# A 34th slot for weight pieces and their high parts, and DMA scratch of 256 bytes

## The chip, the cores and the metric

The kernel runs on one core of a Trainium2 chip. The metric is the device time of one execution in microseconds (us). The kernel before took 749.93 us, the median of three runs (749.84 to 750.58). Every time below is of the kernel before.

## What is computed

An attention layer whose keys are limited to a local window and a few global positions, followed by a feed-forward layer with a rational activation. All tensors are f32:

```python
# q, k, v: (4 batches, 8 heads, 768 positions, 64)
rel = pos[:, None] - pos[None, :]
is_global = pos[None, :] < 8
is_local = (rel >= 0) & (rel < 96)
scores = q @ k.T / 8 - slope[head] * dist        # dist = |rel|, or 96 where only global
a = softmax(where(is_global | is_local, scores, -1e9))
x = (a @ v), heads side by side                  # 3072 tokens x 512
h = x @ w_in                                     # 512 x 2048
P = a0 + a1*h + a2*h**2 + a3*h**3
Q = 1 + |b0|*|h| + |b1|*h**2
out = (P / (Q + 1e-6)) @ w_out                   # 2048 x 512
```

## The kernel before

**Tiling.** The 3072 tokens are taken in 12 chunks of 256. A chunk needs 8 attention units (a unit is one block of 128 queries with one pair of heads) and 8 feed-forward steps f (a step is 256 of the 2048 hidden columns, as two halves of 128). Steps f = 0 to 7 belong to the first chunk, f = 8 to 15 to the second, and so on up to 95. Attention runs ahead of the feed-forward by 10 to 13 units, so that in the steady part each turn of the loop holds one attention unit and one feed-forward step of an earlier chunk.

**Two kinds of arithmetic on TensorE.** For the first chunk, TensorE multiplies with the plain f32 weights (h at L263, acc at L342). From the second chunk on, each weight and each activation is split in a high part, rounded to fp32r, and a low part, the remainder, and a product is three fp32r matmuls: high by high, high by low, low by high (h at L271, acc at L347). Attention's later units (u >= 24) use fp32r as well; the earlier ones, and the products with v (o, L520), stay f32.

**Weights.** `w_in` and `w_out` are cut in 32 pieces of 128x512. A piece goes through four stations:

- `fetch` loads its bytes into a raw tile (r).
- `decode` puts it together as f32 in a slot of the pool `wide`: an Abs on ScalarE (L202), a small scaling on GpSimd (L206), two bit operations on VectorE (L207, L209). The result is named `w_..f` in the trace. The table `WSCHED` says in which turn each piece is decoded (turns 0 to 16).
- `split_w` rounds it into a second slot of `wide`, `w_..h` (L222): every even one on VectorE, every odd one on ScalarE.
- `split_w` then subtracts (L223) and stores the low part in `win_l` or `wout_l`, which have room of their own. This runs on GpSimd, and for ten of the pieces on VectorE.

**The slots.** `wide` has `NCT * DF // (2 * TOK) + NFT + 1` = 16 + 16 + 1 = 33 slots of 128x512 f32, handed out in turn. 32 pieces and 32 high parts pass through them in the order in which the code asks: pieces 0 to 29, the high parts of 0 and 1, pieces 30 and 31, then the high parts of 2 to 31. So piece 31 takes the slot of piece 0, and the high part of piece n (n >= 2) the slot of piece n-1. It may be written only when everything that reads piece n-1 is done: the f32 matmuls of the first chunk and the subtraction of L223. The high part of n+1 waits in the same way for piece n, and so on: one chain through all pieces. The pieces' order is that of `WSCHED`: (1,2,0), (1,3,0), (1,0,0), (1,1,0), (1,2,1), (1,3,1), (1,0,1), (1,1,1) of `w_in`, then rows 0 to 3 of `w_out`, and so on to row 15.

**What sets the order of the work.** Every group of instructions has a priority: its turn, and within the turn a number from a table (`PRI`, in the first turns `PRI_A`). Splits come last in their turn (`wsplit`). A list scheduler with a timing model then lays down each engine's queue: at each point it takes the group of best priority among those which the model says can start. The queues are in order on the chip, so an instruction that waits holds up everything behind it on its engine.

**The feed-forward step on the engines.** h (TensorE) -> three activations from h (ScalarE, L295 to L297: fu, fa, fs) -> fu times h twice (VectorE, L302, L303) and fa + fs (GpSimd, L304) -> log and exp (ScalarE, L311, L312) -> three operations (VectorE, L316 to L318), whose last gives fu. In the first chunk acc (L342) reads fu. After it, ScalarE rounds fu into g (L326), GpSimd stores the remainder in g (L327), and acc (L347) reads g. The PSUM tiles of h are two, so the h of f waits until L303 of f-2 is done. GpSimd also scales the probabilities (L478, two for each unit).

**DMA scratch.** `dynamic_dma_scratch_size` keeps 2048 bytes of each partition of SBUF for transfers whose descriptors software makes.

## Time and profile before

| what | value |
|---|---|
| median of 3 runs | 749.93 us |
| the profiled execution | 750.29 us |
| its span, first to last instruction | 748.4 us |
| outside the span | 1.9 us |
| mean granted TensorE clock | 0.996 |
| TensorE busy, matmuls | 724.8 us |
| splits, high parts (L222) | 32, from 75.7 to 177.2 us |
| splits, low parts (L223) | 22 on GpSimd, 10 on VectorE, from 80.2 to 178.9 us |

The splits thus fill the second and third tenth of the execution. Up to about 115 us TensorE works on the first chunk in f32; the steady part with its three fp32r matmuls for each product begins near 140 us and goes on to the end. A matmul's record lasts longer than its share of the array, since one begins before the other has drained: what TensorE spends on it is read from one start to the next.

### The profile page before, as it was taken

The numbers are of one execution on the slowest core, as the hardware profiler recorded it, in microseconds if no ns is written. First come the engines' busy times: TensorE is split into PE (matmuls) and PEld (weight loads), VectorE is DVE, ScalarE is ACT, GpSimd is POOL, SyncE is SP. The second block draws the span as 40 slices with busy tenths as digits, with TensorE's granted clock in tenths as the row PEclk, the third lists the DMA queues.
The fourth block names the chain that finished last, engine by engine and source line by source line (L and its number), as shares of the span: only waits on it lengthen the run. The fifth ranks groups of instructions, "written<-read, shape, count | busy, mean of one in ns | idle before, by whom it ended". The sixth has DMA issues, their size and how long they took to land.

```text
span 748.4 us, 15330 instructions
## 1 busy us (share of the span) xinstructions
PE 724.8 (97%) x5026; PEld 629.8 (84%) x5026; DVE 601.4 (80%) x1437; ACT 576.9 (77%) x1303; POOL 456.4 (61%) x504
## 2 busy tenths in 40 slices
PE   5898999999999999999999999999999999999996
PEld 4575667888988989999999999998988989998995
DVE  5889965888889797878888888887888888876565
ACT  6898576977987886877877878777877877866674
POOL 3384996776576675665756657656666566664441
PEclk9999999999999999999999999999999999999999
DMA  9986101123534443334434334334434333210000
GB/s 259 306 277 224 48 22 23 50 52 99 146 103 126 151 121 94 113 108 101 119 94 120 113 101 125 107 101 106 124 93 124 117 86 107 74 50 1 29 1 33
DMA packets 123581, 79.49 MB, mean 106 GB/s; under 512 B 82532, under 2 KB 104036, under 8 KB 123492
## 3 DMA queue, kind: packets, MB, share of 16 engines
q1 hardware_dynamic: 122288, 77.89, 36.4%
q8 instruction: 42, 0.69, 0.4%
q10 hardware_dynamic: 1204, 0.52, 0.3%
q14 instruction: 47, 0.39, 0.2%
HBM read 35.92 MB, written 6.29 MB: 56 GB/s over the span
## 4 chain that ended last, share of the span: by engine, by line
PE 90%; DVE 3%; DMA 3%; ACT 1%; issue 1%; SPq 0%; POOL 0%; DVEq 0%; ACTq 0%
PE h L271 34%; PE acc L347 32%; PE o L520 5%; PE s L438 5%; PE tp L494 4%; PE acc L342 3%; PE h L263 3%; PE s L433 2%; PE tk L383 1%; DMA r<-in_moe_w_in_dram 1%; DMA r<-in_moe_w_out_dram 1%; PE tk L389 1%; DMA nat<-in_q_dram 0%; DVE pr L452 0%; ACT pr L462 0%
## 5 line engine op out<-in xcount | busy, mean ns | idle before, releaser
L478 POOL TENSOR_SCALAR pr<-pr,stats 128x256 f32<-128x256 f32 (+1 forms) x176 | 156.3, 899 | 74.8 <-DVE stats L469 42.7
L271 PE MATMUL h<-xh,win_l 128*128 128x256 f32 x704 | 198.2, 282 | 0.0
L304 POOL TENSOR_TENSOR fa<-fa,fs 128x512 f32<-128x512 f32 x95 | 123.5, 1300 | 98.0 <-ACT fs L297 85.3
L347 PE MATMUL acc<-wout_l,g 128*128 128x512 f32 x352 | 139.3, 396 | 0.0
L271 PEld LDWEIGHTS h<-xh,win_l 128*128 128x128 f32 x704 | 133.1, 189 | 2.1 <-issue 1.2
L327 POOL TENSOR_TENSOR g<-fu,g 128x512 fp32r<-128x512 f32 x87 | 113.9, 1310 | 34.2 <-ACT g L326 22.8
L295 ACT ACTIVATE fu<-h,coef 128x512 f32<-128x512 f32 (+1 forms) x97 | 74.9, 772 | 45.0 <-PE h L271 39.8
L462 ACT ACTIVATE pr<-pr,stats 128x256 f32<-128x256 f32 (+1 forms) x192 | 92.9, 487 | 16.8 <-DVE stats L452 16.0
L311 ACT ACTIVATE fs<-fa,coef 128x512 f32<-128x512 f32 (+1 forms) x97 | 69.6, 718 | 30.0 <-POOL fa L304 28.4
L316 DVE SCALAR_TENSOR_TENSOR fu<-fu,coef,q 128x512 f32<-128x512 f32 (+1 forms) x97 | 71.6, 738 | 24.7 <-ACT q L312 23.3
L302 DVE TENSOR_TENSOR fu<-fu,h 128x512 f32<-128x512 f32 (+1 forms) x97 | 65.7, 677 | 30.5 <-ACT fs L297 27.9
L347 PEld LDWEIGHTS acc<-wout_l,g 128*128 128x128 f32 x352 | 66.2, 188 | 11.9
L415 ACT ACTIVATE kq<-tk 64x256 fp32r<-64x256 f32 x144 | 54.2, 377 | 26.6 <-DVE kq L416 15.1
L303 DVE SCALAR_TENSOR_TENSOR fu<-fu,coef,h 128x512 f32<-128x512 f32 (+1 forms) x97 | 71.7, 739 | 2.0
L317 DVE SCALAR_TENSOR_TENSOR q<-fa,coef,q 128x512 f32<-128x512 f32 (+1 forms) x97 | 72.1, 744 | 0.0
L497 DVE COPY pT<-tp 128x512 f32<-128x512 f32 (+1 forms) x75 | 48.4, 646 | 26.0 <-PE tp L494 25.1
L416 DVE SCALAR_TENSOR_TENSOR kq<-tk,kq 64x256 fp32r<-64x256 f32 x144 | 60.8, 423 | 8.6 <-ACT kq L415 4.2
L318 DVE SCALAR_TENSOR_TENSOR fu<-q,fu 128x512 f32<-128x512 f32 (+1 forms) x97 | 66.1, 682 | 1.6
L297 ACT ACTIVATE fs<-h,coef 128x512 f32<-128x512 f32 (+1 forms) x97 | 66.2, 683 | 1.5 <-DMA out_dram<-o 1.2
L296 ACT ACTIVATE fa<-h,coef 128x512 f32<-128x512 f32 (+1 forms) x97 | 65.5, 675 | 0.4 <-DMA out_dram<-o 0.4
L326 ACT CAST g<-fu 128x512 fp32r<-128x512 f32 (+1 forms) x89 | 54.9, 617 | 8.5 <-DVE fu L318 7.8
L312 ACT ACTIVATE q<-fs 128x512 f32<-128x512 f32 (+1 forms) x97 | 57.3, 591 | 2.2 <-DVE fu L318 0.7
(258 smaller groups left out, 2006.1 us busy)
## 6 DMA issues: line engine op xcount, KB each, us to landing
pm<-pr SPq DMA_DIRECT2D x60, 256.0 KB
mv<-nat SPq DMA_DIRECT2D x36, 256.0 KB
qT<-kq SPq DMA_DIRECT2D x144, 64.0 KB
r<-in_moe_w_in_dram SPq DMA_DIRECT2D x16, 512.0 KB
r<-in_moe_w_out_dram SPq DMA_DIRECT2D x16, 512.0 KB
nat<-in_q_dram SPq DMA_DIRECT2D x48, 128.0 KB
vt<-in_v_dram SPq DMA_DIRECT2D x48, 128.0 KB
nat<-in_k_dram SPq DMA_DIRECT2D x46, 128.0 KB
```

What stands on the lines that cost most here:

```text
L271: nc.tensor.matmul(out=hps[f][:, y, :], lhsT=w[:, fs], rhs=x[:, ct, :], start=(n == 0), stop=(n == 3 * NCT - 1))
L295: nc.scalar.activation(out=u, in_=h, func=AF.Identity, scale=a3, bias=a2)
L297: nc.scalar.activation(out=s, in_=h, func=AF.Square, scale=b1)
L303: nc.vector.scalar_tensor_tensor(out=u, in0=u, scalar=a1, in1=h, op0=ALU.add, op1=ALU.mult)
L304: side(f).tensor_tensor(out=a, in0=a, in1=s, op=ALU.add)
L311: nc.scalar.activation(out=s, in_=a, func=AF.Ln, bias=q1)
L316: nc.vector.scalar_tensor_tensor(out=u, in0=u, scalar=a0, in1=r, op0=ALU.add, op1=ALU.mult)
L317: nc.vector.scalar_tensor_tensor(out=r, in0=a, scalar=q1, in1=r, op0=ALU.add, op1=ALU.mult)
L327: side(f).tensor_tensor(out=g[:, 1, ys], in0=u, in1=g[:, 0, ys], op=ALU.subtract)
L347: nc.tensor.matmul(out=acc, lhsT=gs[f][:, z, y, ts], rhs=w, start=(ft == 0 and n == 0), stop=(ft == NFT - 1 and n == 2))
L462: nc.scalar.activation(out=d, in_=d, func=AF.Exp, scale=-1.0, bias=st[:, x:x + 1], accum_out=st[:, 2 + 2 * x:3 + 2 * x])
L478: nc.gpsimd.tensor_scalar(out=d, in0=d, scalar1=st[:, 6 + x:7 + x], scalar2=None, op0=ALU.mult)
```

## The change

`wide` gets one slot more, 34, and the DMA scratch shrinks from 2048 to 256 bytes of each partition. A slot takes 2048 bytes of each partition, so the 34th needs most of what the scratch gives back (1792) and 256 more.

```diff
     def piece(dt, key):
         return wide.tile([P, 2 * TOK], dt, tag="w", name=f"w{'_'.join(map(str, key))}{'f' if dt is F32 else 'h'}",
-                         bufs=NCT * DF // (2 * TOK) + NFT + 1)
+                         bufs=NCT * DF // (2 * TOK) + NFT + 2)
...
-    nc = _bacc.Bacc("TRN2", target_bir_lowering=False, num_devices=1, dynamic_dma_scratch_size=2048)
+    nc = _bacc.Bacc("TRN2", target_bir_lowering=False, num_devices=1, dynamic_dma_scratch_size=256)
```

In the same order of requests, piece 31 now takes a slot that nothing has used, and the high part of piece n (n >= 2) takes the slot of piece n-2. No instruction is added or removed. But the scheduler now sees the splits as ready earlier, and lays down other queues from there on: TensorE's queue differs from 91 us of the trace of before onwards, in many places up to the last chunks, VectorE's from 86 us, ScalarE's from 80 us, GpSimd's from 89 us, and SyncE's from its 98th row of transfers.

VectorE's queue where it first differs; rows with - stood there before, rows with + stand there now (w_..h are high parts, w_..f decoded pieces, fu, q and fa tiles of feed-forward steps, r raw tiles; the numbers tell tiles of one name apart, fu_840 being step 3 and fu_925 step 4):

```order
 L302 TENSOR_TENSOR fu_925<-fu_925,h_905 128x512
-L467 TENSOR_REDUCE stats<-stats 128x2
 L209 SCALAR_TENSOR_TENSOR w_15f<-r_15_1115,w_15f 128x512
+L467 TENSOR_REDUCE stats<-stats 128x2
+L222 CAST w_2_1h<-w_2_1f 128x512
 L318 SCALAR_TENSOR_TENSOR fu_840<-q_916,fu_840 128x512
 L303 SCALAR_TENSOR_TENSOR fu_925<-fu_925,coef,h_905 128x512
 L469 RECIPROCAL stats<-stats 128x2
-L222 CAST w_2_1h<-w_2_1f 128x512
+L222 CAST w_0_1h<-w_0_1f 128x512
```

The high part of piece 4 (w_2_1h) moves ahead of the last operation of step 3, and the place that it had goes to piece 6.

GpSimd's queue at the same time (pr are probabilities of attention units, win_l low parts of w_in):

```order
 L440 COPY kF<-kGF 128x8
 L478 TENSOR_SCALAR pr_898<-pr_898,stats 128x256 x2
+L223 TENSOR_TENSOR win_l<-w_1_0f,w_1_0h 128x512
+L223 TENSOR_TENSOR win_l<-w_0_0f,w_0_0h 128x512
 L304 TENSOR_TENSOR fa_926<-fa_926,fs_927 128x512
-L223 TENSOR_TENSOR win_l<-w_0_0f,w_0_0h 128x512
-L223 TENSOR_TENSOR win_l<-w_1_0f,w_1_0h 128x512
+L223 TENSOR_TENSOR win_l<-w_3_1f,w_3_1h 128x512
+L223 TENSOR_TENSOR win_l<-w_2_1f,w_2_1h 128x512
 L440 COPY kF<-kGF 128x8
 L478 TENSOR_SCALAR pr_966<-pr_966,stats 128x256 x2
```

Two low parts now stand ahead of L304 of step 4 instead of behind it, and the low parts of the next two pieces follow ahead of the next probabilities (pr_966).

TensorE's queue near 213 us, the product with v of units 24 to 27 (o_2510; acc are output sums of the third chunk, vt tiles of v):

```order
+L520 MATMUL o_2510<-pT_2200,vt_1788 64x128 x2
+L347 MATMUL acc_0_2250<-w_4h,g_2370 128x512
+L520 MATMUL o_2510<-pT_2279,vt_1788 64x128
+L347 MATMUL acc_0_2250<-w_5h,g_2370 128x512
+L520 MATMUL o_2510<-pT_2279,vt_1788 64x128
+L347 MATMUL acc_0_2250<-wout_l,g_2370 128x512
+L520 MATMUL o_2510<-pT_2326,vt_1987 64x128
+L347 MATMUL acc_0_2250<-w_5h,g_2370 128x512
+L520 MATMUL o_2510<-pT_2326,vt_1987 64x128
+L520 MATMUL o_2510<-pT_2417,vt_1987 64x128 x2
```

Before, these eight products stood in one stretch, ahead of the first four matmuls of acc; now four matmuls of acc stand among them and cut the stretch in five.

## The prediction

> **What bounds the kernel now.** I read the page first, then the stretches of time, then TensorE's waits.

> ```profile
> PE 724.8 (97%) x5026; PEld 629.8 (84%) x5026; DVE 601.4 (80%) x1437; ACT 576.9 (77%) x1303; POOL 456.4 (61%) x504
> ```

> The matmuls (PE) are busy for 97% of the span; VectorE (DVE), ScalarE (ACT) and GpSimd (POOL) have room. A share over the whole span hides stages, so I cut the span where the change can act: up to 91 us TensorE's queue is the same in both kernels, from 91 to 141 the splits are dense, from 141 to 181 they run out, and then comes the steady part. The columns are the busy time of each engine, with its instructions, then TensorE's clock and the DMA engines' share.

> ```profile
> core 0: us, PE busy (x) PEld busy (x) DVE busy (x) ACT busy (x) POOL busy (x), PEclk, DMA share, GB/s
> 70.00:91.00 21.00, 18.29 (x69) 11.66 (x69) 21.00 (x39) 12.58 (x28) 16.86 (x15) 0.92 0.32 112
> 91.00:141.00 50.00, 49.79 (x271) 35.88 (x270) 35.72 (x82) 38.52 (x90) 38.50 (x39) 1.00 0.12 30
> 141.00:181.00 40.00, 40.00 (x274) 33.86 (x272) 34.64 (x75) 32.02 (x72) 30.25 (x27) 1.00 0.25 59
> 181.00:700.00 519.00, 518.40 (x3860) 471.38 (x3859) 427.64 (x1028) 407.47 (x899) 319.20 (x348) 1.00 0.37 103
> ```

> TensorE is idle for 2.7 us between 70 and 91, and for less than 0.9 us in the 609 us after that. Its waits say the same (what waited, for whom; us in total, times, longest), first from 70 to 91, then from 91 to the end:

> ```profile
> PE acc L342 <- DVE fu L318: 3.6, 1, 3.6
> PE h L263 <- DVE fu L303: 1.1, 1, 1.1
> ...
> PE s L438 <- DVE pT L497: 0.4, 1, 0.4
> PE acc L342 <- DVE fu L318: 0.2, 1, 0.2
> PE tp L494 <- DVE stats L452: 0.2, 1, 0.2
> ```

> So the two large waits lie ahead of the place where the queues part, and **behind it there is 0.8 us of waiting in all**. What the change can win on TensorE is at most that.

> **What the change removes.** It removes the wait of a high part for the low part of the piece before it. Who waited for L223:

> ```profile
> who waited for it (us, times):
>   DVE w_0h L222: 2.3, 1
>   DVE w_1h L222: 1.6, 2
>   DVE w_2h L222: 1.2, 2
> ```

> These are the largest; all lie on VectorE, with ScalarE's smaller, at times when both have over 20% to spare (91 to 141), and TensorE behind them stood still for 0.2 us (the wait on L318, below). Their disappearance is worth nothing on the path: the cover is TensorE's own queue, full from 91 us on. If that cover had holes, they would be in the second list above, and it has none of size.

> **The scratch.** It matters to transfers that software describes. The queues of this execution:

> ```profile
> q1 hardware_dynamic: 122288, 77.89, 36.4%
> q8 instruction: 42, 0.69, 0.4%
> q10 hardware_dynamic: 1204, 0.52, 0.3%
> q14 instruction: 47, 0.39, 0.2%
> ```

> All data goes through hardware queues, so I count the smaller scratch as nothing, from either side.

> **What the change moves.** No instruction comes or goes, 5026 matmuls stay 5026. Three things can still cost.

> *First, one wait at 92 us.* VectorE now makes the high part w_2_1h ahead of L318 of step 3, and that high part takes the slot of piece 2 (w_0_0f), whose low part is now the second L223 behind the probabilities on GpSimd. The rows of before there:

> ```profile
> 88.58 1.51 POOL L304 TENSOR_TENSOR fa<-fa,fs 128x512 f32<-128x512 f32 x1
> 90.06 1.27 POOL L223 TENSOR_TENSOR win_l<-w_0f,w_0h 128x512 fp32r<-128x512 f32 x1
> 91.80 0.68 DVE L318 SCALAR_TENSOR_TENSOR fu<-q,fu 128x512 f32<-128x512 f32 x1
> 93.38 0.43 DVE L222 CAST w_1h<-w_1f 128x512 fp32r<-128x512 f32 x1 [0.17 <-POOL win_l L223]
> 92.53 1.12 PE L342 MATMUL acc<-w_6f,fu 128*128 128x512 f32 x2 [0.21 <-DVE fu L318]
> ```

> From 88.6 on, two L223 of 1.27 to 1.5 us end at 91.1 to 91.6. VectorE had been due at L318 at 91.80, with the same instructions ahead of it but for the cast of 0.43 (0.34 from start to start). So L318 begins 0.2 to 0.4 us later, and TensorE, which waits for just this tile, loses **+0.3 us** (range 0 to 0.6).

> *Second, the seams of TensorE's queue.* Counted in the two queues from 91 us on, the products with v (L520) stand in 37 stretches in place of 32; five seams more, four of them at units 24 to 27. What a seam costs, from rows of before:

> ```profile
> 143.42 0.39 PE L347 MATMUL acc<-w_2h,g 128*128 128x512 f32 x1
> 143.65 0.40 PE L347 MATMUL acc<-wout_l,g 128*128 128x512 f32 x1
> 143.98 0.44 PE L520 MATMUL o<-pT,vt 128*64 128x128 f32 x4
> 144.35 0.33 PE L494 MATMUL tp<-ident,pr 128*128 128x128 f32 x1
> ...
> 212.68 1.09 PE L520 MATMUL o<-pT,vt 128*64 128x128 f32 x16
> 213.70 0.50 PE L347 MATMUL acc<-w_4h,g 128*128 128x512 f32 x1
> 214.04 0.39 PE L347 MATMUL acc<-wout_l,g 128*128 128x512 f32 x1
> ```

> From start to start, acc takes 0.23 us before another acc (143.42 to 143.65) and 0.33 before an o (143.65 to 143.98): +0.10. Sixteen o in one stretch take 1.02 us (212.68 to 213.70), 0.064 each; four of them alone take 0.37 (143.98 to 144.35) in place of 0.26: +0.11. That makes 0.21 for a seam, and 0.1 more where two acc follow the o (213.70 to 214.04 is 0.34). Five seams: **+1.1 us** (0.8 to 1.6). The other kinds change their stretches too (h 209 to 216, acc 160 to 168, early s 11 to 10, late s 88 to 92, tp 92 in both). Among the fp32r kinds a seam shows little; I take 0 for them, between -0.5 (fewer of the early f32 seams) and +0.3.

> *Third, the splits pack into the dense stage.* The last high part on ScalarE moves from the first of these rows to right behind the second, some 40 us earlier:

> ```profile
> 176.60 0.62 ACT L222 CAST w_15h<-w_15f 128x512 fp32r<-128x512 f32 x1
> 135.74 0.27 ACT L404 COPY kF<-tk 128x128 f32<-128x128 f32 x1
> ```

> With it nearly all splits of 141 to 181 come ahead of 141. Their sizes, by the stretches of time for L223 alone:

> ```profile
> core 0: us, DVE busy (x) POOL busy (x), PEclk, DMA share, GB/s
> 91.00:141.00 50.00, 3.58 (x5) 18.18 (x15) 1.00 0.12 30
> 141.00:181.00 40.00, 4.71 (x5) 6.45 (x5) 1.00 0.25 59
> ```

> GpSimd's load between 91 and 141 grows from 38.5 to 45.0 us of 50. Its L304 of step 4 comes 2.5 us later (two L223 ahead of it), which reaches L318 of step 4 and the acc that reads it. Step 4's rows of before:

> ```profile
> 96.39 0.68 DVE L318 SCALAR_TENSOR_TENSOR fu<-q,fu 128x512 f32<-128x512 f32 x1
> 99.72 1.02 PE L342 MATMUL acc<-w_8f,fu 128*128 128x512 f32 x2
> ```

> There are 2.65 us between the end of L318 (97.07) and the matmul, which itself now stands some 1 us later in the queue. The cover holds, by about a microsecond, so I take 0 here. Ends: nothing, and the price of the first rival. What the emptier stage of 141 to 181 gains is worth nothing, since TensorE is busy for all of its 40 us.

> **The sum.** 0.3 + 1.1 = 1.4 us, made against the profiled execution: its 750.29 us (span 748.4 and 1.9 around it) become 751.7. The median of the runs shown lies 0.36 lower, 749.93, so the forecast is **751.3 us**, +0.19%. About 0.2% (1.5 us) is what a measurement of this kernel can tell from no change; the forecast lies just inside.

> **Rivals.**

> *GpSimd becomes the bound of the dense stage (slower).* Place: L304 of steps 4 to 8 behind low parts. It decides once L304 comes more than about 3.5 us later than now, 2.65 plus the matmul's own delay. For it: the first L223 were slow, and casts on VectorE beside a busy GpSimd too:

> ```profile
> L223 POOL TENSOR_TENSOR win_l<-w_0f,w_0h x4: 1272/1436/1803, 80.2 to 92.1; 128x512 fp32r<-128x512 f32 x4
> 141.53 1.43 DVE L222 CAST w_3h<-w_3f 128x512 fp32r<-128x512 f32 x1
> ```

> With 1.8 in place of 1.27 for two L223 and 1.43 in place of 0.43 for one cast, step 4 is 2 us later still than reckoned, 4.5 in all, so TensorE waits 1 us there, and perhaps once more in steps 5 to 8: 751.3 + 1 to 2, or **752.8 us**. Against it: the slack grows with the steps.

> [...]

> *The waits go and the seams are free (faster).* The 0.8 us of waits vanish and seams cost nothing, since TensorE could make up time elsewhere: **749.1 us**. Against it: seams are read off the trace, and TensorE has nothing to make up. For 748.4 or less it would need a gain that this trace doesn't show.

> *The slot binds nothing that counts, and the new order is as good as the old*: **749.9 us**. The queues show that the splits do move, so it would be luck of the order.

> **How the numbers follow.** Forecast (751.3, own range 750.5 to 752.0) 0.50; GpSimd late (752 to 754) 0.28; waits gone 0.14; no difference 0.08. The 8 in 10 range runs from half of the faster cases to most of the slow one: 749.5 to 753.3. Slower by over 0.2% (above 751.43): nearly all of the slow rival and 0.15 of the forecast's upper end, 0.42. Faster by over 0.2% (below 748.43): half of the faster rival, 0.07. Within: 0.51.

> **What would show it.** In the profile after: splits done near 145 us, and no wait of L222 for L223 beyond 1 us (the change does what it says); acc w_6f waiting 0.4 to 0.6 us for L318 (first step); the o of units 24 to 27 taking some 0.2 us more for each seam (second); acc w_8f without a wait (third), or with one of about 1 us (the first rival); after 141 us no wait above 0.5 us. I'd be wrong if TensorE shows waits behind 181 us that before did not have, in the thousands of instructions whose order I have not followed one by one, or if its idle time between 70 and 91 us changes.

## The result and the profile after

The changed kernel takes **757.21 us** (median of 6 runs, 756.82 to 758.61), beside 750.29 us of the kernel before on the same chip (6 runs, 749.84 to 751.20): ratio 1.0096, 95% interval 1.0083 to 1.0109. The forecast was 751.3 us and its range ended at 753.3, so some 6 us are missing from its sum. The profiled execution of the changed kernel took 757.04 us, with a span of 755.2; that is 6.75 us more than the profiled execution before, and it is these that the traces have to account for.

TensorE's line of the page first:

```profile
PE 727.3 (96%) x5026; PEld 631.1 (84%) x5026; DVE 605.2 (80%) x1436; ACT 577.9 (77%) x1304; POOL 458.3 (61%) x504
```

2.5 us of the loss is busy time (724.8 before), the rest is idle. (A page's busy time counts the records, which overlap: the four o at 216.90 us of the changed kernel last 0.44 us, and the next matmul starts 0.36 after the first of them. What a matmul costs is read further down, from one start to the next.) The four stretches of time that the prediction used, in the changed kernel:

```profile
core 0: us, PE busy (x) PEld busy (x) DVE busy (x) ACT busy (x) POOL busy (x), PEclk, DMA share, GB/s
70.00:91.00 21.00, 17.35 (x58) 11.67 (x59) 21.00 (x37) 12.21 (x29) 18.36 (x16) 0.92 0.33 110
91.00:141.00 50.00, 47.58 (x253) 32.96 (x252) 44.41 (x87) 37.24 (x87) 43.02 (x40) 1.00 0.12 30
141.00:181.00 40.00, 40.00 (x271) 34.52 (x270) 28.37 (x67) 31.38 (x70) 25.12 (x24) 1.00 0.22 54
181.00:700.00 519.00, 517.38 (x3847) 468.98 (x3847) 424.34 (x1026) 405.94 (x898) 317.79 (x348) 1.00 0.37 104
```

Between 91 and 141 us TensorE is now idle for 2.4 us (before 0.2). GpSimd went from 38.5 to 43.0 us of 50, which the prediction had expected, but VectorE went from 35.7 to 44.4, which it had not looked at. TensorE's waits in the changed kernel, first from 70 to 91 us, then from 91 us to the end:

```profile
PE acc L342 <- DVE fu L318: 3.1, 1, 3.1
PE h L263 <- DVE fu L303: 2.8, 1, 2.8
...
PE h L271 <- DVE fu L303: 1.1, 1, 1.1
PE s L433 <- ACT kF L404: 1.0, 1, 1.0
PE acc L342 <- DVE fu L318: 1.0, 1, 1.0
PE o L520 <- DVE stats L452: 0.5, 1, 0.5
PE tp L494 <- DVE stats L452: 0.3, 1, 0.3
```

Behind 91 us 0.8 us of waiting have become 3.9. To see where the loss arises, I looked for points of the program where both queues have issued the same set of matmuls, and compared the start of the next matmul in the two traces, both counted from their first matmul. How late TensorE is against before, at the last such point at or ahead of each time (times of before; worked out from the 5026 matmul records of each trace):

```
us of before                  87    97   113   136   158   207   219   250   259   end
change                       1.0   1.8   1.4   2.7   3.6   4.1   5.4   5.4   6.7   6.6
change, second profile       0.9   1.6   1.3   2.6   3.6   4.0   5.3   5.3   6.6   6.6
```

**The loss arises in four stretches: 1.8 us by 97 us, another 1.8 from there to 158 (and 0.5 more by 207, without a single wait of size), and 1.3 each near 217 and 259 us.** Behind that nothing changes for 480 us. The second line is another profile of the same kernel; it repeats the first within 0.2 us. Steps of 0.4 us from one column to the next mean little: the next matmul need not be of the same kind in both queues (1.4 at 113 is such a place; points beside it give 1.8 and 2.1), and at 136 the last point lies just ahead of a wait.

*By 97 us.* Rows of the changed kernel, VectorE, GpSimd and TensorE by their start:

```profile
91.10 1.07 DVE L209 SCALAR_TENSOR_TENSOR w_15f<-r,w_15f 128x512 int32<-128x512 int32 x1
91.59 1.71 POOL L223 TENSOR_TENSOR win_l<-w_1f,w_1h 128x512 fp32r<-128x512 f32 x1
92.16 1.43 DVE L222 CAST w_1h<-w_1f 128x512 fp32r<-128x512 f32 x1
93.51 0.68 DVE L318 SCALAR_TENSOR_TENSOR fu<-q,fu 128x512 f32<-128x512 f32 x1
94.25 1.12 PE L342 MATMUL acc<-w_6f,fu 128*128 128x512 f32 x2 [1.04 <-DVE fu L318]
```

The cast that the new order puts ahead of L318 takes 1.43 us, not the 0.43 of the row at 93.38 us of before, which had no low part beside it, while a low part runs on GpSimd (an experiment below takes that low part away). L318 starts at 93.51 (before: 91.80), 1.71 us later, and that is TensorE's lateness here. The cast accounts for 1.35 of it, from its start to that of L318; VectorE was late by the other 0.36 already, and ahead of that a bit operation (L209 of w_14f) took 1.75 us beside two low parts, in place of 0.68. TensorE also waited longer for L303 in the stretch ahead of it (2.8 us, before 1.1) and ran the next matmuls at half clock (0.61 from 82 to 86 us), but since it waits for L318 afterwards anyway, this doesn't add to it.

*From 97 to 158 us.* The costliest chain, with GpSimd, ScalarE and TensorE:

```profile
134.53 1.28 POOL L223 TENSOR_TENSOR wout_l<-w_12f,w_12h 128x512 fp32r<-128x512 f32 x1
135.77 1.28 POOL L304 TENSOR_TENSOR fa<-fa,fs 128x512 f32<-128x512 f32 x1
137.08 0.72 ACT L311 ACTIVATE fs<-fa,coef 128x512 f32<-128x512 f32 x1 [1.39 <-POOL fa L304]
139.51 0.27 ACT L404 COPY kF<-tk 128x128 f32<-128x128 f32 x1
139.83 1.13 PE L433 MATMUL s<-kF,qz 128*128 128x256 f32 x4 [1.04 <-ACT kF L404]
```

A low part stands ahead of fa of step 9; ScalarE waits for fa with everything that is queued behind L311, kF among it, and TensorE's scores wait for kF. With a wait of 0.3 us for VectorE just ahead (tp), that is 1.4 of the 1.8 us.

*Near 217 us.* The products with v (L520) between 200 and 300 us, grouped by line, first before, then changed: busy us and mean ns of one.

```profile
L520 PE MATMUL o<-pT,vt 128*64 128x128 f32 x112 | 7.0, 276 | 0.0
```

```profile
L520 PE MATMUL o<-pT,vt 128*64 128x128 f32 x112 | 8.3, 278 | 0.5 <-DVE stats L452 0.5
```

The same 112 matmuls show 1.3 us more of busy time, since they stand in more stretches: this figure tells whether an order has the seams, but not what they cost. That is read from one start to the next, first in the changed kernel, then the row that ends the place in the kernel before:

```profile
216.90 0.44 PE L520 MATMUL o<-pT,vt 128*64 128x128 f32 x4
217.26 0.50 PE L347 MATMUL acc<-w_4h,g 128*128 128x512 f32 x1
217.70 0.43 PE L520 MATMUL o<-pT,vt 128*64 128x128 f32 x2
220.66 0.50 PE L347 MATMUL acc<-w_4h,g 128*128 128x512 f32 x1
```

```profile
214.74 0.28 PE L438 MATMUL s<-kq 128*128 128x256 f32 x1
```

Sixteen o and four acc take 3.76 us now (216.90 to 220.66) and took 2.06 before (212.68 to 214.74): 1.7 us for four seams, 0.43 each. The lateness grows by 1.3 only, so the new order gives some 0.4 back around them, at places that I haven't followed.

*Near 259 us.* Rows of the changed kernel:

```profile
255.64 1.83 POOL L478 TENSOR_SCALAR pr<-pr,stats 128x256 f32<-128x256 f32 x2 [1.71 <-ACT fs L311]
257.15 0.42 DVE L452 CUSTOM_DVE_ANT_0 pr<-s,masks 128x256 f32<-128x256 f32 x1 [1.67 <-POOL pr L478]
257.85 0.68 DVE L302 TENSOR_TENSOR fu<-fu,h 128x512 f32<-128x512 f32 x1
260.94 0.75 DVE L303 SCALAR_TENSOR_TENSOR fu<-fu,coef,h 128x512 f32<-128x512 f32 x1
261.75 0.39 PE L271 MATMUL h<-xh,w_1h 128*128 128x256 f32 x1 [1.12 <-DVE fu L303]
```

H of step 27 needs the PSUM buffer that L302 and L303 of step 25 read. On VectorE these two now stand behind an L452 that waits 1.67 us for GpSimd, with four other instructions between them. In the kernel before they came first, close together, and the L452 after them:

```profile
250.43 0.69 DVE L302 TENSOR_TENSOR fu<-fu,h 128x512 f32<-128x512 f32 x1 [1.05 <-ACT fs L297]
251.61 0.75 DVE L303 SCALAR_TENSOR_TENSOR fu<-fu,coef,h 128x512 f32<-128x512 f32 x1
252.27 0.42 DVE L452 CUSTOM_DVE_ANT_0 pr<-s,masks 128x256 f32<-128x256 f32 x1
```

The splits themselves are where the prediction put them. The last high part and the last low part, behind which no L223 follows:

```profile
139.67 0.62 ACT L222 CAST w_15h<-w_15f 128x512 fp32r<-128x512 f32 x1
140.81 0.68 DVE L223 TENSOR_TENSOR wout_l<-w_15f,w_15h 128x512 fp32r<-128x512 f32 x1
```

### The profile page after: what moved, and what is told of

It reads as the page before. It is cut to its first block, busy times and chain, and to the rows that moved or that the text cites. A ratio compares the mean times of both kernels' runs of the same rounds, so it can differ in the third digit from the quotient of the medians.

```text
span 755.2 us, 15321 instructions
## 1 busy us (share of the span) xinstructions
PE 727.3 (96%) x5026; PEld 631.1 (84%) x5026; DVE 605.2 (80%) x1436; ACT 577.9 (77%) x1304; POOL 458.3 (61%) x504
## 3 DMA queue, kind: packets, MB, share of 16 engines
q1 hardware_dynamic: 122288, 77.89, 36.1%
q10 hardware_dynamic: 1204, 0.52, 0.3%
## 4 chain that ended last, share of the span: by engine, by line
PE 82%; DVE 7%; ACT 5%; DMA 2%; POOL 1%; issue 1%; SPq 0%; DVEq 0%; POOLq 0%; ACTq 0%
PE acc L347 32%; PE h L271 31%; PE o L520 5%; PE s L438 4%; PE tp L494 3%; PE h L263 2%; PE s L433 2%; DMA r<-in_moe_w_in_dram 1%; PE tk L383 1%; ACT pr L462 1%; DVE pr L452 1%; DVE fu L303 1%; DVE fu L302 1%; DVE q L317 1%; ACT qz L402 1%
## 5 line engine op out<-in xcount | busy, mean ns | idle before, releaser
L304 POOL TENSOR_TENSOR fa<-fa,fs 128x512 f32<-128x512 f32 x95 | 124.3, 1308 | 97.9 <-ACT fs L297 84.2
L347 PE MATMUL acc<-wout_l,g 128*128 128x512 f32 x352 | 139.5, 396 | 0.0
L302 DVE TENSOR_TENSOR fu<-fu,h 128x512 f32<-128x512 f32 (+1 forms) x97 | 65.7, 677 | 34.5 <-ACT fs L297 33.6
L311 ACT ACTIVATE fs<-fa,coef 128x512 f32<-128x512 f32 (+1 forms) x97 | 69.7, 718 | 26.3 <-POOL fa L304 24.8
L347 PEld LDWEIGHTS acc<-wout_l,g 128*128 128x128 f32 x352 | 66.2, 188 | 11.7 <-issue 0.2
L303 DVE SCALAR_TENSOR_TENSOR fu<-fu,coef,h 128x512 f32<-128x512 f32 (+1 forms) x97 | 71.7, 739 | 2.0
L497 DVE COPY pT<-tp 128x512 f32<-128x512 f32 (+1 forms) x75 | 48.4, 646 | 24.8 <-PE tp L494 24.1
L318 DVE SCALAR_TENSOR_TENSOR fu<-q,fu 128x512 f32<-128x512 f32 (+1 forms) x97 | 66.1, 682 | 1.5
```

The source lines that it names most:

```text
L302: nc.vector.tensor_tensor(out=u, in0=u, in1=h, op=ALU.mult)
L303: nc.vector.scalar_tensor_tensor(out=u, in0=u, scalar=a1, in1=h, op0=ALU.add, op1=ALU.mult)
L304: side(f).tensor_tensor(out=a, in0=a, in1=s, op=ALU.add)
L311: nc.scalar.activation(out=s, in_=a, func=AF.Ln, bias=q1)
L347: nc.tensor.matmul(out=acc, lhsT=gs[f][:, z, y, ts], rhs=w, start=(ft == 0 and n == 0), stop=(ft == NFT - 1 and n == 2))
```

## The experiments

Four theories stood at the start, and the expectations speak of them by number. **1**: the splits, packed into 80 to 141 us, get in the way of the chains there. **2**: any new order of the queues costs some us by chance, wherever it comes from. **3**: the half-clock stretch near 85 us is chance of the run. **4**: the smaller scratch, or the addresses that 34 slots bring, cost time by themselves. The times are medians; the ratio, to before on the same chip, is worked out from the single runs and can differ from that of the medians by up to 0.1%.

### Is it the order, or the scratch and the slots themselves?

Scratch alone:

```diff
- nc = _bacc.Bacc("TRN2", target_bir_lowering=False, num_devices=1, dynamic_dma_scratch_size=2048)
+ nc = _bacc.Bacc("TRN2", target_bir_lowering=False, num_devices=1, dynamic_dma_scratch_size=256)
```

> 33 slots as before, only the DMA scratch of 256 bytes. The instructions of every engine stand in the order of before. Theory 1 (the loss comes from the splits standing earlier in the dense stage between 80 and 141 us) and theory 2 (any new order of the same work costs some us by chance): 749.9 to 750.7 us, ratio 1.000. Theory 3 (the 1 us lost at 82 to 86 us, where the h matmuls of step 5 ran at half clock, is chance of the run): same time, but the matmuls L263 of step 5 may show either form, 0.22 or 0.43 us each. Theory 4 (scratch and addresses cost time by themselves): over 751.5 us.

Measured: 750.24 us, ratio 1.0003 (0.9993 to 1.0012).

The change, with a spare tile that takes one slot just ahead of piece 31 and gives it back behind fu of step F (F = 90, 6 and 8 in the three kernels):

```diff
-     hi = {}
+     hi = {}; spare = []
...
-         dst = full[key] = piece(F32, key)
+         dst = full[key] = (len(full) == 31 and spare.append(piece(F32, (9, 9))) or spare and len(full) == 31 and nc.gpsimd.memset(spare[0][:, 0:1], 0.0) and None, piece(F32, key))[1]
...
+         if f == F and spare: nc.gpsimd.tensor_tensor(out=spare[0][:, 0:1], in0=spare.pop()[:, 0:1], in1=u[:, 0, 0:1], op=ALU.add)
```

> 34 slots and scratch of 256, but a spare tile of the same shape holds the 34th slot to the end of the program (one 1-column memset and one 1-column add on GpSimd more), so that every high part again takes the slot of the piece just before it and TensorE's order is that of before. Theories 1 and 2: 749.9 to 750.9 us, with TensorE's waits of before. Theory 4 (the addresses that 34 slots bring): over 751.5 us, up to 757.

Measured: 750.30 us, ratio 1.0003 (0.9993 to 1.0012). Its waits of TensorE from 91 us on are those of before:

```profile
PE s L438 <- DVE pT L497: 0.4, 1, 0.4
PE tp L494 <- DVE stats L452: 0.2, 1, 0.2
PE acc L342 <- DVE fu L318: 0.2, 1, 0.2
```

Theory 4 falls: scratch and addresses cost nothing that can be measured (under 0.12%, the end of the interval). **The time is lost by what the free slot does to the order.**

> 34 slots; the spare tile gives its slot back behind fu of step 6. TensorE's order is that of before up to about 132 us, and o of L520 has 32 stretches as before; on GpSimd 19 low parts stand ahead of fa (L304) of step 9, where the change has 21. Theory 1: no loss at 92 us, no wait of acc w_6f over 0.5 us; the loss between 111 and 141 us stays in part, 0.8 to 2 us; no loss at 205 to 217 us: 751.0 to 753.0 us. Theory 2: a new order of its own, losses of 0 to 3 us at places that have nothing to do with low parts, most of them behind 141 us: 750.5 to 753.5 us. Telling: where TensorE loses it, and what it waited for.

> 34 slots; the spare tile gives its slot back behind fu of step 8. 16 low parts stand ahead of fa (L304) of step 9 on GpSimd (change: 21), TensorE's order is that of before up to about 144 us, and o has 35 stretches in place of 32. Theory 1: none of the losses before 141 us; three more seams of about 0.2 to 0.3 us: 750.7 to 751.5 us. Theory 2: 750.5 to 753.5 us, the more the earlier the order parts from that of before, so less than held_to_step6.

Measured: 751.79 us, ratio 1.0023 (1.0013 to 1.0032), and 751.45 us, 1.0016 (1.0007 to 1.0026). Held to step 8, TensorE loses nothing ahead of 141 us; it has these two waits behind 91 us,

```profile
PE h L271 <- DVE xl L550: 0.4, 1, 0.4
PE acc L347 <- ACT g L326: 0.4, 1, 0.4
```

and its 2.2 us at the end of the trace (the profiled run took 752.49, 1 us more than the median) go with the seams and small waits of a third order (L520 shows 8.1 us between 200 and 300). Held to step 6, the loss of 92 us is gone, that near 136 us is there with the same wait of s for kF (0.8 us), and L520 shows 7.0 us. So the two losses ahead of 158 us come and go with how early the slot is free, as theory 1 has it, and those behind it don't.

### Does it repeat, and which engine is in the way?

> The change itself once more, to see which of its five losses repeat. Theories 1 and 2: the losses at 92 us (acc w_6f), near 136 us (scores of tile 20 behind kF), at 205 to 217 us (o cut by acc) and near 258 us (h of step 27 behind fu L303) stand in the trace again within 0.3 us each, 757 us. Theory 3: the half-clock stretch need not lie on h of step 5 at 83 to 86 us; if it lies on acc at 71 to 77 us as in before, TensorE is about 1 us nearer to before at 86 us and the time is 755.5 to 756.5 us; if it lies on h again, it belongs to the new order and not to chance.

Measured: 756.84 us in one run; all places repeat, as the second line of the first table shows, and so does the half clock at 82 to 86 us (0.62, in the first profile 0.61). That doesn't decide theory 3, since the steps at which the clock changes (last section) lie at the same place in both profiles, within 0.1 us. The sum doesn't need it: TensorE waits for L318 behind the half-clock stretch in any case.

Every high part on VectorE, first with the change, then with the 33 slots and the scratch of before:

```diff
- HI_V = (0, 2, 4, 6, 8, 10, 12, 14, 16, 18, 20, 22, 24, 26, 28, 30)
+ HI_V = tuple(range(32))
```

> The change with every high part (L222) on VectorE, none on ScalarE, so that no cast can hold ScalarE's queue. o has 37 stretches as in the change. Theory 1 in the form that ScalarE's queue is held by casts whose slot is not free (8.4 us of such waits behind 76 us in the change): the waits of ScalarE for L223 go to 0, the losses at 92 and 136 us shrink by 0.5 to 1.5 us together, 755 to 756.5 us. Theory 1 in the form that GpSimd itself is late: nothing gained, VectorE has 16 casts of 0.4 us more in the stage, 757 to 759 us. Theory 2: 755 to 759 us, no telling.

> 33 slots and scratch of 2048 as before, but every high part (L222) on VectorE. The order of TensorE parts from before at about 91 us, as in the change, and o has 37 stretches as in the change, though each high part still takes the slot of the last piece. Theory 1: the splits stay late, so no loss near 92 and 136 us but for VectorE's 16 casts of 0.4 us; the five seams cost 1.1 to 1.6 us and the wait near 258 us may come: 751.5 to 753.5 us. Theory 2 (the order, not the slots, costs the time): as much as the change, 755 to 758 us.

The low parts of the even pieces on VectorE:

```diff
- LO_V = (13, 15, 17, 19, 21, 23, 25, 27, 29, 31)
+ LO_V = tuple(range(0, 32, 2))
```

> The change with the low parts L223 of the 16 even pieces on VectorE and of the 16 odd ones on GpSimd (change: 22 on GpSimd, 10 on VectorE). On GpSimd 15 low parts stand ahead of fa (L304) of step 9 in place of 21, and 7 in place of 14 ahead of that of step 7; o has 37 stretches. Theory 1 with GpSimd late: the wait near 136 us (s behind kF) is gone or under 0.3 us and acc w_6f waits under 0.5 us: 1 to 2.5 us less, 754.5 to 756 us. Theory 1 with the queue of ScalarE held: the casts wait less too, the same sign but 756 to 757 us. Theory 2: 755 to 759 us.

Measured: casts on VectorE 761.39 us, ratio 1.0167 (1.0147 to 1.0187); the same with 33 slots 754.61, 1.0069 (1.0045 to 1.0092); low even on VectorE 759.76, 1.0144 (1.0127 to 1.0161). Both kernels with 34 slots, which load VectorE further, are slower than the change, and slower than any time that had been expected of them. I had believed that ScalarE's queue was the culprit, since its casts wait in the changed kernel:

```profile
ACT w_1h L222 <- POOL win_l L223: 2.7, 1, 2.7
ACT w_0h L222 <- POOL win_l L223: 2.4, 1, 2.4
ACT w_9h L222 <- DVE wout_l L223: 1.8, 1, 1.8
ACT w_3h L222 <- POOL wout_l L223: 1.5, 1, 1.5
```

With no cast on ScalarE the gain was to be 0.5 to 1.5 us, and 4 us were lost. That form of theory 1 falls. The other half of the guess, that fewer low parts on GpSimd help, fails where they go to VectorE instead. VectorE is what both had more of, 46.0 and 47.3 us of 50 in the dense stage; here is that stretch with the even low parts on VectorE, and its longest wait:

```profile
91.00:141.00 50.00, 45.74 (x236) 31.16 (x236) 47.29 (x91) 35.51 (x80) 38.26 (x34) 1.00 0.10 26
```

```profile
PE tp L494 <- DVE stats L452: 2.8, 1, 2.8
```

The run with the old slots is the telling one for the other half: it has 33 slots and hardly a loss between 97 and 158 us (0.5), but at 219 and 259 us it loses 1.3 us each, as the change does (2.2 us late at 207, 3.5 at 219, 4.8 at 259). **So these 2.6 us belong to an order that the change happens to bring, and that can be had without it.** Its 754.61 us lie between the two expectations, 1.1 above theory 1's: the 2.2 us lost by 207 us had been put lower.

### One low part at a time

```diff
- LO_V = (13, 15, 17, 19, 21, 23, 25, 27, 29, 31)
+ LO_V = (5, 13, 15, 17, 19, 21, 23, 25, 27, 29, 31)
```

> The change with one low part more on VectorE: that of piece 5 (w_3_1), which ran on GpSimd at 91.6 to 93.3 us beside the cast w_1h of VectorE (1.43 us). TensorE's order differs from the change in 22 places between 99 and 108 us and nowhere else. If the loss at 92 us is VectorE slowed beside GpSimd's low part: the cast takes about 0.4 us, L318 of step 3 starts about 1 us earlier, acc w_6f waits under 0.3 us, 756.2 to 756.7 us. If the cast is slow for another reason or the loss comes from ScalarE's held queue: acc w_6f waits 1.0 us again, 757 us. In both, the losses at 136, 217 and 258 us stay as they are.

Measured: 756.04 us, ratio 1.0082 (1.0058 to 1.0105). VectorE's rows there:

```profile
92.36 0.41 DVE L222 CAST w_1h<-w_1f 128x512 fp32r<-128x512 f32 x1
92.70 0.68 DVE L318 SCALAR_TENSOR_TENSOR fu<-q,fu 128x512 f32<-128x512 f32 x1
```

The same cast takes 0.41 in place of 1.43 us once that low part is gone from beside it, L318 starts 0.8 us earlier, and TensorE is 1.1 us late at 97 us in place of 1.8. So the low part beside it is what lengthens the cast, and that is worth 0.7 of the 1.8 us. What is left is the cast's own 0.34 us and VectorE's lateness ahead of it, 0.5 us here, with L209 of w_14f again at 1.75 us beside two low parts. The time alone wouldn't show it, since the two ratios' intervals overlap, and acc w_6f still waited 1.7 us (I had written under 0.3): TensorE came to it earlier in this run.

Three further edits put 26, 4, or both into LO_V in the same way.

> The change with one low part more on VectorE: that of piece 26 (w_10). TensorE's order differs from the change only between about 139 and 160 us; on ScalarE kF (L404) of tile 20 now stands ahead of L311, on GpSimd one low part less stands ahead of fa (L304). If the wait of 1.0 us near 136 us comes from kF standing on ScalarE behind L311, which waits for the late fa of GpSimd: no such wait, 755.6 to 756.4 us. If it comes from the packed VectorE: the wait moves to tp or h and is as long or longer, 756.8 to 758.5 us. The losses at 92, 217 and 258 us stay.

> The change with one low part more on VectorE: that of piece 4 (w_2_1). 34 slots, and the splits as packed as in the change, but TensorE's order is word for word that of before from about 184 us on, with 32 stretches of o. If the losses at 205 to 217 us and near 258 us (2.7 us together) belong to the order of that part alone: both gone, 754.0 to 755.2 us, with L520 at 7.0 us between 200 and 300 us. If they belong to the early splits (buffers or transfers that come earlier): still there, 756.5 to 757.5 us.

> Both: low parts of pieces 4 and 26 on VectorE. 34 slots, TensorE's order that of before from about 184 us on. If the causes add up: 753.0 to 754.2 us, with what is left of the loss before 141 us. If VectorE's queue becomes the bound of the dense stage: a wait of tp, h or acc of 1.5 to 3 us between 110 and 141 us and 755 to 757 us.

Measured: 26 on VectorE 756.93 us (1.0099, 1.0075 to 1.0124), 4 on VectorE 755.18 (1.0075, 1.0048 to 1.0103), both 756.01 (1.0078, 1.0056 to 1.0101). With 26 the wait for kF is indeed gone, but h waits 0.5 us and tp 0.6 in its place, and from 97 to 158 us 1.9 us are lost as before: the chain was named rightly and was not the only one, as the second half of the expectation had it. With 4, the tail has the order of before and loses nothing behind 185 us, with 34 slots and early splits: the other side of the experiment with the old slots. It gains only 2 us by that, because of a third thing near 94 us:

```profile
93.79 1.29 PE L342 MATMUL acc<-w_6f,fu 128*128 128x512 f32 x2 [2.73 <-DVE fu L318]
94.87 1.91 PE L342 MATMUL acc<-w_7f,fu 128*128 128x512 f32 x2
96.58 1.75 PE L342 MATMUL acc<-w_6f,fu 128*128 128x512 f32 x2
98.16 1.02 PE L342 MATMUL acc<-w_7f,fu 128*128 128x512 f32 x2
```

TensorE came earlier, waited 2.7 us for the same late L318, and then ran at half clock (0.58 from 94 to 98 us): 1.7 us lost that the change spends at 85 us, where it is covered. The same happens with 4 and 26 together (a wait of 2.4 us), and with late casts on ScalarE and more low parts on GpSimd (2.5 and 2.6 us, then a clock of 0.57 and 0.63 from 94 to 98 us), the two kernels that follow: 1.7 us of their lateness of 3 to 4.4 us at 97 is this. With 4 and 26 together, the wait of 1.5 to 3 us that the expectation puts between 110 and 141 us isn't there, though the time falls in its range.

### VectorE or GpSimd in the dense stage?

```diff
- HI_V = (0, 2, 4, 6, 8, 10, 12, 14, 16, 18, 20, 22, 24, 26, 28, 30)
+ HI_V = (0, 2, 4, 6, 8, 10, 12, 14)
```

> The change with the 8 even high parts from 16 on made by ScalarE in place of VectorE. TensorE's order is that of the change up to about 130 us and that of before from about 184 us on. On VectorE 16 splits stand ahead of L318 of step 8 (change: 25), on GpSimd 20 low parts ahead of fa of step 9 (change: 21). If VectorE is the bound of the dense stage: busy 41 us or less of 91 to 141 (change: 44.4), no wait near 136 us over 0.4 us, the loss there under 0.8 us; with 1.8 us lost by 92 us and none at 217 and 258 us 751.8 to 753.2 us. If GpSimd is the bound: the wait near 136 us stays, 754 to 755.5 us.

```diff
- LO_V = (13, 15, 17, 19, 21, 23, 25, 27, 29, 31)
+ LO_V = (13, 15, 17, 19, 21)
```

> The change with 5 low parts on VectorE and 27 on GpSimd (change: 10 and 22). TensorE's order is that of the change up to about 130 us and that of before from about 184 us on. On GpSimd 24 low parts stand ahead of fa of step 9 (change: 21), on VectorE 20 splits ahead of L318 of step 8 (change: 25). If VectorE is the bound of the dense stage: the loss at 111 to 141 us falls under 1 us, 752 to 753.5 us. If GpSimd is the bound: it grows to 3 us or more, 754.5 to 757 us.

The first of these with low part 5 on VectorE as well:

> The change with the even high parts from 16 on made by ScalarE, and the low part of piece 5 on VectorE. TensorE's order is that of before from about 184 us on. If each cause was found: the cast ahead of L318 of step 3 takes 0.4 us (loss at 92 us 1.1 in place of 1.8 us), little is lost at 136 us, nothing at 217 and 258 us: 751.0 to 752.5 us. It beats before (750.3 us) in neither theory, since 0.8 us is all that TensorE waits for behind 91 us there. If VectorE is not the bound: 753.5 us or more.

Measured: 756.34 us (1.0092, 1.0070 to 1.0113), 757.19 (1.0094, 1.0077 to 1.0112) and 754.31 (1.0059, 1.0042 to 1.0075). How late TensorE was in all of them, and VectorE's and GpSimd's busy time of the 50 us from 91 to 141. The table is of the profiled run of each kernel, which differs from the median by up to 1.1 us:

```
us of before                  87    97   113   136   158   207   219   259   end   DVE  POOL
held to step 8               0.8   0.5   0.5   0.5   0.2   0.2  -0.1   0.6   2.2  36.3  38.9
old slots, casts on vector   1.3   0.8   0.9   1.1   1.3   2.2   3.5   4.8   4.8  38.3  36.2
held to step 6              -0.2  -0.4  -0.4  -0.5   0.4   0.9   0.9   0.9   0.9  40.5  42.7
late casts on scalar        -0.7   3.2   2.9   3.5   4.3   5.4   5.4   5.4   5.4  39.2  40.0
more low on GpSimd           0.5   4.4   4.0   4.7   6.0   7.0   7.0   7.0   7.0  40.3  44.7
both relieved                0.3   1.6   1.3   2.0   3.5   4.0   4.0   4.0   4.0  41.3  40.9
low 4                       -1.2   3.0   2.7   3.0   4.7   5.1   5.1   5.1   5.1  44.5  41.6
low 26                       0.3   1.1   0.7   2.2   3.0   3.4   4.7   6.1   6.0  44.8  41.6
low 4 and 26                -0.5   3.4   3.0   3.9   4.8   5.2   5.2   5.3   5.2  45.3  41.0
low 5                       -0.4   1.1   0.7   2.2   3.2   3.6   4.9   6.3   6.2  45.4  43.0
change                       1.0   1.8   1.4   2.7   3.6   4.1   5.4   6.7   6.6  44.4  43.0
low even on vector           0.0   0.2   0.4   4.8   5.4   5.8   7.1   8.6   8.5  47.3  38.3
casts on vector              0.3   0.5   1.0   6.7   8.2   8.6   9.9  11.2  11.1  46.0  42.2
```

Neither forecast of the stage held. From 97 to 158 us, late casts on ScalarE lose 1.1 us and more low on GpSimd 1.6, where the change loses 1.8; both relieved lose 1.9. The loss isn't gone in any of them, and the wait has another name each time (h for L303 0.8 us in the first; s for kF 1.1 us in the second, as if GpSimd were late; h for L303 1.6 us where both are relieved). What the table does show: kernels with up to 38 us of VectorE's work in the stage lose at most 0.5 us there, those with 39 to 45 between 0.8 and 2.1, those with 46 and 47 about 8 and 5 (in the first of them a wait of 3.8 us for L303 and the half clock behind it, 0.58 from 142 to 146 us, are part of that). **That the early splits cost 0.8 to 2.1 us in the dense stage, and more where VectorE gets more of them, is shown, by two kernels with late splits against eleven with early ones; that one engine alone bounds it is not**, and I leave that open. All three lose nothing between 207 and 259 us, with L520 at 7.0 us, as their order foretold. No kernel here beats before. Both relieved takes 754.31 us in place of the 751.0 to 752.5 that would have meant that each cause was found.

## Why the prediction was wrong

- **What can be won: right.** Behind 91 us there was nothing to win, and scratch and slots by themselves are worth nothing (1.0003 each).
- **What the change does: right, but for one line.** The splits are done at 141.5 us. "No wait of L222 for L223 beyond 1 us" was wrong: the waits left VectorE and came back on ScalarE, 1.5 to 2.7 us each.
- **The first step, +0.3 us: right place, wrong size.** L318 of step 3 was priced with the cast at 0.34 us, from a row that had no low part beside it. It took 1.43 beside a low part on GpSimd, ending 0.3 us after it, and by 97 us TensorE had lost 1.8. Low part 5 taken off GpSimd shows it for the cast (0.41 us, 0.7 us less lost); what is left came from VectorE being late ahead of it, which the prediction didn't reckon. The prediction had the row of 1.43 us in its hands, and used it for the rival and not for the sum. That was the mistake, since the cast that counts was the new one ahead of L318. By what means a low part lengthens a cast, no run here shows.
- **The second step, +1.1 us: right place, and the size came out by luck.** TensorE loses 1.3 us near 217 us, within the 0.8 to 1.6 given. But a seam cost 0.43 us there, twice the 0.21 of the sum: an acc that stands alone among o is followed after 0.44 us in place of the 0.33 reckoned (217.26 to 217.70), and two o alone take 0.36. Four seams are 1.7 us, of which the order around them gives 0.4 back.
- **The third step, taken as 0: the step that failed.** It lost 1.8 us from 97 to 158 and 0.5 more by 207. Acc w_8f did not wait, as said; but the argument looked at step 4 and at GpSimd alone. GpSimd came to 43.0 us (45.0 had been reckoned); VectorE, whose share of the packed splits was never counted, came from 35.7 to 44.4, so that "over 20% to spare" no longer held. The packed splits got into chains that feed other matmuls than this acc, those of tp and of the scores, and cost 1.8 us of TensorE's time; which engine bounds that stage stays open. The first rival named the mechanism (fa behind low parts) with 1 to 2 us. It came at step 9, not 4 to 8, through ScalarE's queue to the scores; "the slack grows with the steps" speaks of acc alone and didn't protect them.
- **Not in the sum: h of step 27, +1.3 us.** The prediction said that it would be wrong if waits came up behind 181 us, in the part of the order that had not been followed. That is what happened. It was also to be wrong if the idle time between 70 and 91 us changed; it did (2.7 to 3.65 us), but L318 decides there anyway.

The sum as it came out: 1.8 + 1.8 + 0.5 + 1.3 + 1.3 = 6.7 us, of which 1.4 had been counted. The 0.5 us between 158 and 207 us have no wait behind them and stay unexplained.

## What to carry to other kernels

Price a moved instruction by the rows that will stand beside it, not by rows from another place (the cast took 1.43 us beside a low part and 0.41 without), and count the load of every engine on which the moved work lands. Where a scheduler lays the queues, a freed buffer can change their order to the end of the program: follow the new queue row by row as far as it differs, since 2.6 of the 6.7 us here came over 60 us after the last split, from an order that also arises without it.

## What the runs showed that was not expected

TensorE's clock fell after some waits. In the changed kernel the 2.8-us wait for L303 is followed by this (the columns are the length, TensorE's busy time, its clock, the DMA engines' share and GB/s):

```profile
78.00:82.00 4.00, 1.53 (x11) 1.00 0.29 66
82.00:86.00 4.00, 3.67 (x10) 0.61 0.00 0
```
